# A gated recurrence and a two-layer network on one core: units 4 and 5 also run the first layer 512 columns wide, with a new order of all steps

## The chip, the cores and the metric

The kernel runs on one core of a Trainium2 chip. TensorE (PE) multiplies matrices, with its weight loads shown as an engine of their own (PEld); VectorE (DVE), ScalarE (ACT) and GpSimd (POOL) do element-wise work; SyncE (SP) issues nearly all DMAs. The metric is device time in microseconds: before the change a median of 175.93 us over 3 runs (175.39 to 175.97).

## The reference

Inputs q, k, v and f_logit have the shape (4 batches, 8 heads, 768 steps, 48). For each batch and head a 48 x 48 state is kept, and y is read from it at each step; then a two-layer network with a leaky ReLU runs over the 3072 tokens of 384 values:

```python
f = 1.0 / (1.0 + np.exp(-f_logit))
for t in range(S):
    state = f[:, :, t, :, None] * state + np.einsum('bhd,bhe->bhde', k[:, :, t], v[:, :, t])
    y[:, :, t] = np.einsum('bhd,bhde->bhe', q[:, :, t], state)
x = y.transpose(0, 2, 1, 3).reshape(B * S, H * D)
h = x @ w_in                       # 384 -> 2048
out = np.maximum(0.01 * h, h) @ w_out   # 2048 -> 384
```

## The kernel before

Time is cut into 6 chunks of 128 steps, and the work into 12 units of 256 tokens. Units 0 to 3 are one batch each with its chunks 0 and 1; units 4 to 11 are one chunk of two batches. Units 4 and 5 are chunk 2 of the four batches, 6 and 7 chunk 3, and so on.

For each unit the following is done. f, k, q and v are loaded (in the order's short names `Lf`, `Lk`, `Lq`, `Lv`, two halves each). ACT makes the log of the gate (`ge`, `gl`), PE its cumulative sum (`cs`), ACT the decay factors for k and q (`dec`, tiles em and at). k and q are scaled by them (`k`, `q`, on DVE or POOL; the last number of the word is 0 for DVE and 1 for POOL), v is cast (`v`). k and q are turned by PE with a copy behind (`tk`, `tq`, `ck`, `cq`, units 0 to 3) or by a transposing DMA on SP's queue (`xk`, `xq`, units 4 to 11). PE makes the scores (`sc`), DVE masks them (`mk`, four for a unit, tile wm), PE mixes with v and the old state (`mx`, `ms`), and two copies bring the result to the tile xT (`xt`). The new state goes through PE (`pt`), DVE (`sf`) and POOL (`sb`).

The network follows on xT. The first layer of a unit is 8 groups `up`: each does two of 16 blocks of 128 hidden values, in 2 x 3 matmuls of 256 columns (line 523), and ACT empties the bank through the leaky ReLU into the tile gT (`pr`, line 528). For two units at once it is 16 groups `uw` of 3 matmuls of 512 columns (line 534), each with one emptying of the same 128x512 size (`pv`, line 537). Which pairs do this, `WIDE` says; units 6 to 9 do so before the change. The layout of xT and gT follows it. The second layer is four quarters `dn` of 4 matmuls for each half of a unit (line 544), a copy to one of four output buffers (`ob`) and a store (`st`). Unit 11's second half ends in two half-width parts (`dc`, line 566).

Weights are loaded as f32 in eight parts each (`WI`, `WO`) into the raw buffers of units 4 and 5, and cast (`ci`, `co`). `F` words are matmuls on zeros, which fill PE's waits at the start; `Z` and `M` words clear and make constants. PSUM has eight banks; the number behind `@` is a word's bank.

Nothing is scheduled by a planner at build time. A string of words, written out in the kernel, is the order: each engine runs its instructions in the order of these words, and waits on semaphores for what they need. So an instruction that waits holds up all that stand behind it on its engine, and a DMA that waits on SP's queue holds up all later loads and stores.

Of the kernel before, what the change touches and what calls it, by code (L numbers as in the profile page):

```python
# [704 lines left out]
```

## Time and profile before

| | us |
|---|---|
| median of 3 runs | 175.93 |
| profiled execution, whole | 176.14 |
| its span | 173.9 |
| PE busy | 166.8 |
| ACT busy | 112.3 |
| DVE busy | 84.3 |
| POOL busy | 71.2 |
| PE's idle time that waits for DVE's scaling of k, in all | 1.2 |

Busy times are of the profiled execution and leave out issuing and waiting. A busy PE isn't PE at its peak: a matmul's length in the profile holds the depth of its pipeline, and what counts for the stream is the step from one start to the next.

### The profile page before, as it was taken

The numbers are of one execution on the slowest core, as the hardware profiler recorded it, in microseconds if no ns is written. First come the engines' busy times: TensorE is split into PE (matmuls) and PEld (weight loads), VectorE is DVE, ScalarE is ACT, GpSimd is POOL, SyncE is SP. The second block draws the span as 40 slices with busy tenths as digits, with TensorE's granted clock in tenths as the row PEclk, the third lists the DMA queues.
The fourth block names the chain that finished last, engine by engine and source line by source line (L and its number), as shares of the span: only waits on it lengthen the run. The fifth ranks groups of instructions, "written<-read, shape, count | busy, mean of one in ns | idle before, by whom it ended". The sixth has DMA issues, their size and how long they took to land.

```text
span 173.9 us, 5261 instructions
## 1 busy us (share of the span) xinstructions
PE 166.8 (96%) x2163; PEld 114.3 (66%) x2167; DVE 84.3 (48%) x159; ACT 112.3 (65%) x214; POOL 71.2 (41%) x127
## 2 busy tenths in 40 slices
PE   7878899999999999999999999999999999999993
...
PEclk9999999999999999999999999999999999999999
...
GB/s 138 320 312 323 329 245 374 357 156 260 293 210 180 198 153 210 179 250 217 182 138 188 243 153 216 165 172 195 216 210 140 230 185 185 73 94 45 0 94 92
DMA packets 109192, 34.45 MB, mean 198 GB/s; under 512 B 101872, under 2 KB 108144, under 8 KB 109168
## 3 DMA queue, kind: packets, MB, share of 16 engines
...
## 4 chain that ended last, share of the span: by engine, by line
PE 89%; DVE 3%; DMA 3%; ACT 1%; issue 1%; SPq 1%; DVEq 0%; ACTq 0%
PE ps L544 35%; PE ps L523 24%; PE ps L534 12%; PE ps L419 6%; DMA k_raw<-in_k_dram 3%; PE ps L388 3%; PE ps L269 2%; PE ps L566 2%; PE ps L345 1%; PE ps L495 1%; PE ps L381 1%; PE ps L101 1%; SPq L209 1%; DVE vb L328 1%; PE ps L490 1%
## 5 line engine op out<-in xcount | busy, mean ns | idle before, releaser
L544 PE MATMUL ps<-w_out,gT 128*128 128x384 bf16 x368 | 66.1, 326 | 0.0
L544 PEld LDWEIGHTS <-gT 128*128 128x128 bf16 x368 | 34.6, 98 | 22.6
L528 ACT ACTIVATE gT<-ps 128x512 bf16<-128x512 f32 x64 | 35.6, 615 | 16.3 <-PE ps L523 15.7
L523 PE MATMUL ps<-xT,w_in 128*128 128x256 bf16 x384 | 44.4, 273 | 0.2 <-DVE w_in L175 0.2
L523 PEld LDWEIGHTS <-w_in 128*128 128x128 bf16 x384 | 37.2, 98 | 5.9 <-DVE w_in L175 0.5
L402 DVE TENSOR_TENSOR wm<-ps,ut 128x512 bf16<-128x512 f32 x32 | 19.9, 684 | 17.6 <-PE ps L388 17.4
L537 ACT ACTIVATE gT<-ps 128x512 bf16<-128x512 f32 x32 | 17.6, 615 | 6.9 <-PE ps L534 6.9
L534 PE MATMUL ps<-xT,w_in 128*128 128x512 bf16 x92 | 21.8, 379 | 0.2
L324 POOL TENSOR_TENSOR kh<-k_raw,em 128x384 bf16<-128x384 f32 (+1 forms) x8 | 10.3, 1283 | 24.2 <-DMA end<-at 12.1
L324 DVE TENSOR_TENSOR kh<-k_raw,em 128x384 bf16<-128x384 f32 (+1 forms) x8 | 8.1, 1009 | 17.0 <-DMA k_raw<-in_k_dram 11.4
L534 PEld LDWEIGHTS <-w_in 128*128 128x128 bf16 x96 | 9.3, 98 | 10.2
L515 POOL CAST sb<-sf 64x192 bf16<-64x192 f32 x40 | 14.6, 364 | 3.3 <-DVE sf L505 0.9
L307 ACT ACTIVATE em<-ps 128x384 bf16<-128x384 f32 x24 | 12.2, 508 | 4.8 <-POOL sb L515 2.0
L512 POOL TENSOR_TENSOR sf<-sf,end 128x192 f32<-128x192 f32 x12 | 8.2, 680 | 16.9 <-DVE qh L324 12.5
L553 ACT COPY osb<-ps 128x384 f32<-128x384 f32 x12 | 5.9, 499 | 14.1 <-PE ps L544 11.2
L240 ACT ACTIVATE f_raw<-f_raw 128x384 f32<-128x384 f32 (+1 forms) x16 | 11.0, 692 | 4.9 <-DMA f_raw<-in_f_logit_dram 4.9
L507 DVE TENSOR_TENSOR sf<-sf,ps 64x192 f32<-64x192 f32 x32 | 11.2, 350 | 5.5 <-POOL qh L321 2.9
L328 POOL CAST vb<-v_raw 128x768 bf16<-128x768 f32 (+1 forms) x10 | 7.6, 762 | 14.2 <-PE ps L388 8.1
L321 POOL TENSOR_TENSOR qh<-q_raw,at 128x768 bf16<-128x768 f32 x4 | 8.7, 2187 | 6.8 <-ACT at L309 4.2
L555 DVE COPY osb<-ps 128x384 f32<-128x384 f32 x11 | 6.0, 555 | 11.2 <-issue 10.1
L252 ACT ACTIVATE lf<-f_raw 128x384 bf16<-128x384 f32 (+1 forms) x16 | 11.1, 691 | 0.4
L479 DVE CAST xT<-ps 128x384 bf16<-128x384 f32 x12 | 6.6, 564 | 9.0 <-PE ps L419 8.9
...
## 6 DMA issues: line engine op xcount, KB each, us to landing
k_raw<-in_k_dram SPq DMA_DIRECT2D x24, 192.0 KB, 3.8
v_raw<-in_v_dram SPq DMA_DIRECT2D x24, 192.0 KB, 3.8
f_raw<-in_f_logit_dram SPq DMA_DIRECT2D x23, 192.0 KB, 3.9
q_raw<-in_q_dram SPq DMA_DIRECT2D x23, 192.0 KB, 4.3
out_dram<-osb SPq DMA_DIRECT2D x23, 192.0 KB, 2.7
...
```

The lines of the kernel that those rows point to most:

```text
L240: nc.scalar.activation(e[:, part], e[:, part], AF.Exp, scale=-1.0)
L252: nc.scalar.activation(dst, src, AF.Ln, bias=1.0)
L307: nc.scalar.activation(ems[j % 2][:, a], t[:, 0:H * D], AF.Exp, scale=1.0)
L324: engine(e).tensor_mul(heads(j, to[j % NR], a)[:, :, :, 0:D], raw_heads(j, x, a), decays(j, by, a))
L402: nc.vector.tensor_mul(w, src.rearrange("t (p n) -> t p n", p=P2), ut[:, None, :].to_broadcast([128, P2, 128]))
L507: nc.vector.tensor_add(sf[rows], sf[rows], new)
L515: nc.gpsimd.tensor_copy(out=sb[rows, :, y * D:y * D + D], in_=sf[rows])
L523: nc.tensor.matmul(pm[:, i, :], w_in_of(ff, kk), xT_of(j)[:, kk].rearrange("t a s -> t (a s)"), start=(kk == 0), stop=(kk == NK - 1))
L528: nc.scalar.activation(gT_of(j)[:, 2 * g:2 * g + 2, :], pm, AF.Prelu, alpha=0.01)
L534: nc.tensor.matmul(banks[bank], w_in_of(ff, kk), x[:, kk], start=(kk == 0), stop=(kk == NK - 1))
L537: nc.scalar.activation(gTs[n % 2][:, 512 * ff:512 * ff + 512], banks[st[2 * n].pop(("pw", ff))], AF.Prelu, alpha=0.01)
L544: nc.tensor.matmul(po, gT_of(j)[:, ff, 128 * a:128 * a + 128], w_out_b[ff // 2][:, ff % 2, :], start=(ff == 0), stop=(ff == NF - 1))
```

## The change

The pair of units 4 and 5 joins `WIDE`: its first layer is 16 groups of 512 columns instead of 16 groups of 2 x 256 columns for the two units, with the matching layout of its xT and gT. The whole order is another one: the same steps in another sequence, on other banks, and partly on other engines. Of the steps on DVE, ACT and POOL, DVE has four more scalings of k and two more of q than before, and POOL that many fewer; ACT casts two input weight parts fewer and one output weight part more. The fill matmuls are 22 of 512 and 5 of 256 columns (20 and 3 before). The words of units 0 to 5 that the prediction speaks of stand in the order below.

```diff
-    WIDE = (3, 4)
+    WIDE = (2, 3, 4)
...
-    Zz Af_1_1 Aq_0_0 F_9_512@6 Lf_0_0 Lf_0_1 Lk_0_1 Lk_0_0 Zb_0_1_0 Zl_2_1 Mi Lv_0_0 Zq_0_0 Lv_0_1 Mu Lq_0_1
...
+    Zz Af_0_1 Ak_0_0 F_9_512@6 Lf_0_0 Lv_0_1 Lq_0_0 Lk_0_1 Lv_0_0 Lq_0_1 Lf_1_1 Lf_2_1 Lf_1_0 Lf_2_0 Lk_1_0
...
```

The loads at the start: before, ACT's queue brings the second half of unit 1's f and the first of unit 0's q, and SP's begins with f, k and v of unit 0. Now ACT's brings the second half of unit 0's f and the first of its k, and SP's begins with f, v, q, k, v, q of unit 0; then come f of units 1 and 2, and the rest of unit 1 ahead of the first weights.

DVE at the start, between the masks of unit 0 (wm0 to wm3) and those of unit 1 (wm4 to wm7). kh and qh are scaled k and q, kT and qT their turned copies, sf the state, w_in5 a part of the input weights. Before:

```order
L398 TENSOR_TENSOR wm3_114<-ps5_144,pair_mask_152 128x512
L360 COPY qT1_110<-ps0_139 128x2x256
L328 CAST vb1_105<-v_raw1_83 128x2x4x48
L324 TENSOR_TENSOR kh1_92<-k_raw1_71,em1_98 128x2x4x48
L328 CAST vb1_105<-v_raw1_83 128x2x4x48
L398 TENSOR_TENSOR wm7_118<-ps6_145,pair_mask_152 128x512
L398 TENSOR_TENSOR wm6_117<-ps5_144,pair_mask_152 128x512
L360 COPY qT1_110<-ps2_141 128x2x256
L505 TENSOR_TENSOR sf1_120<-ps1_140,at1_102 64x192 x2
L398 TENSOR_TENSOR wm4_115<-ps4_143,pair_mask_152 128x512
L175 CAST w_in5_160<-k_raw5_75 128x768
L175 CAST w_in1_156<-k_raw4_74 128x768
```

and with the change:

```order
L324 TENSOR_TENSOR kh1_92<-k_raw1_71,em1_98 128x2x4x48 x2
L507 TENSOR_TENSOR sf0_119<-sf0_119,ps7_146 64x192 x2
L328 CAST vb1_105<-v_raw1_83 128x2x4x48
L360 COPY kT1_108<-ps3_142 128x2x256
L360 COPY qT1_110<-ps5_144 128x2x256
L398 TENSOR_TENSOR wm4_115<-ps6_145,pair_mask_152 128x512
L398 TENSOR_TENSOR wm5_116<-ps7_146,pair_mask_152 128x512
L505 TENSOR_TENSOR sf1_120<-ps0_139,at1_102 64x192 x2
L398 TENSOR_TENSOR wm6_117<-ps5_144,pair_mask_152 128x512
L175 CAST w_in1_156<-k_raw4_74 128x768
L324 TENSOR_TENSOR qh2_96<-q_raw2_78,at2_103 128x2x4x48
L398 TENSOR_TENSOR wm7_118<-ps2_141,pair_mask_152 128x512
```

Both scalings of unit 1's k, the additions to unit 0's state and a scaling of unit 2's q have come into this stretch of DVE's order; one cast of v and the cast of w_in5 have gone out of it, and the first masks of unit 1 (wm4, wm5) stand right behind the copy to qT1.

PE where unit 5's half of the pair begins its first layer, a second-layer matmul ahead of it. Before:

```order
L544 MATMUL ps1_140<-w_out7_170,gT1_134 128x384
L523 LDWEIGHTS w_in1_156
L523 MATMUL ps5_144<-xT0_131,w_in1_156 128x256
L523 LDWEIGHTS w_in1_156
L523 MATMUL ps5_144<-xT0_131,w_in1_156 128x256
```

and with the change:

```order
L544 MATMUL ps1_140<-w_out7_170,gT1_134 128x384
L534 LDWEIGHTS w_in1_156
L534 MATMUL ps4_143<-xT0_131,w_in1_156 128x512
L534 LDWEIGHTS w_in1_156
L534 MATMUL ps4_143<-xT0_131,w_in1_156 128x512
```

The rows before are unit 4's, which stands alone there; unit 5's follow later behind other work. The rows with the change read both units' columns of xT0, so both units' copies into xT0 stand ahead of them.

DVE from the last mask of unit 5 on, with its last copy to xT0 and then unit 6's k, q and v. Before:

```order
L402 TENSOR_TENSOR wm5_116<-ps5_144,ut_153 128x512
L555 COPY osb0_135<-ps7_146 128x384
L479 CAST xT0_131<-ps2_141 128x3x128
L507 TENSOR_TENSOR sf2_121<-sf2_121,ps1_140 64x192 x2
L321 TENSOR_TENSOR qh1_95<-q_raw1_77,at1_102 128x16x48
L507 TENSOR_TENSOR sf3_122<-sf3_122,ps5_144 64x192 x2
```

and with the change:

```order
L402 TENSOR_TENSOR wm7_118<-ps2_141,ut_153 128x512
L555 COPY osb0_135<-ps4_143 128x384
L555 COPY osb2_137<-ps0_139 128x384
L479 CAST xT0_131<-ps5_144 128x3x128
L507 TENSOR_TENSOR sf2_121<-sf2_121,ps3_142 64x192 x2
L555 COPY osb1_136<-ps7_146 128x384
L555 COPY osb3_138<-ps1_140 128x384
L324 TENSOR_TENSOR kh0_91<-k_raw0_70,em0_97 128x16x48
L321 TENSOR_TENSOR qh0_94<-q_raw0_76,at0_101 128x16x48
L507 TENSOR_TENSOR sf3_122<-sf3_122,ps1_140 64x192 x2
L328 CAST vb0_104<-v_raw0_82 128x16x48
```

Two output copies (osb0 of unit 2, osb2 of unit 3) now stand ahead of the copy to xT0; they write the buffers that the stores of units 0 and 1 read. Unit 6's k and v, on POOL before, are on DVE behind two more output copies.

More of the change, by code (lines that the diff above doesn't have):

```diff
@@ L667 @@
[L667 to L669 removed]
+    Zz Af_0_1 Ak_0_0 F_9_512@6 Lf_0_0 Lv_0_1 Lq_0_0 Lk_0_1 Lv_0_0 Lq_0_1 Lf_1_1 Lf_2_1 Lf_1_0 Lf_2_0 Lk_1_0
+    Lq_1_0 Lk_1_1 Lv_1_1 Lv_1_0 Lq_1_1 WI_0 WI_1 Lq_2_1 Zl_0_1 Zb_1_1_0 WI_5 Zq_0_0 Lk_2_1 WI_3 Zb_2_1_1 Mi
+    Ze_1_1 Lq_2_0 WI_2 Zb_2_0_0 Lk_2_0 Lv_2_0 Lv_2_1 WI_4 WI_6 Lf_3_0 WI_7 Zl_2_0 Zl_1_0 Lv_3_1 Lk_3_1 Lf_3_1
@@ new lines @@
+    dec_1_0 k_1_0_0 cs_1_1@5 dec_1_1 k_1_1_0 cs_2_1@6 dec_2_1 Zv_0_1 mx_0_2@0.1 xt_0_0_1 ms_0 xt_0_1_1 cs_2_0@2
+    dec_2_0 sf_0_1 v_1_1_0 tk_1_0@3 ck_1_0_0 tk_1_1@4 ck_1_1_1 q_1_0_1 tq_1_0@5 F_2_512@6 F_1_256@6 cq_1_0_0
+    sc_1_0@6.7 mk_1_0_0 mk_1_0_1 Mt v_1_0_1 pt_1_2@0.3 sf_1_0 q_1_1_1 tq_1_1@1 F_3_512@5 cq_1_1_1 sc_1_1@5.2
+    F_2_512@1 F_1_256@1 ci_0_1 WO_0 up_0_0@6 pr_0_0 mk_1_1_0 ci_1_0 up_0_1@4 WO_1 pr_0_1 sb_1_0 q_2_1_0 tq_2_1@7
+    cq_2_1_1 mk_1_1_1 mx_1_2@1.0 ms_1 xt_1_1_1 ci_5_0 WO_5 up_0_5@5 pr_0_5 k_2_1_1 tk_2_1@6 sf_1_1 sb_1_1
@@ new lines @@
+    xt_1_0_0 up_1_1@2 up_1_5@4 pr_1_5 up_1_0@7 pr_1_1 pr_1_0 ci_3_1 up_1_3@3 up_0_3@1 WO_3 pr_1_3 pr_0_3 q_2_0_0
+    tq_2_0@0 k_2_0_0 tk_2_0@5 ck_2_0_0 ci_2_1 up_1_2@4 WO_2 up_0_2@2 ck_2_1_0 sc_2_1@7.3 mk_2_1_0 mk_2_1_1
+    cq_2_0_1 sc_2_0@1.5 mk_2_0_1 v_2_1_1 pr_0_2 v_2_0_1 pt_2_2@0.6 sf_2_0 ci_4_1 up_1_4@2 pr_1_4 up_0_4@7 WO_4
+    ci_6_1 up_1_6@3 WO_6 up_0_6@5 pr_0_6 mk_2_0_0 mx_2_2@2.0 sb_0_1 xt_2_0_1 pr_0_4 sb_2_0 ms_2 ci_7_0 up_0_7@1
+    pr_0_7 WO_7 up_1_7@5 pr_1_7 xt_2_1_0 up_2_4@2 up_2_1@0 up_2_6@7 up_2_5@1 up_2_3@5 ge_3_1 gl_3_1 pr_1_2
@@ new lines @@
+    dn_1_0_2 co_6_2 Lq_5_1 Lq_5_0 ge_4_2 gl_4_2 cs_4_1@1 cs_4_0@0 dec_4_1 dec_4_0 xe_4 k_4_2_1 xk_4 co_7_0
+    dn_0_0_3 dn_1_0_3 dn_0_1_3 ob_1_0_0 ob_0_0_0 ob_0_1_0 dn_1_1_3 ob_1_1_1 pt_3_2@1.3 sf_3_0 sb_3_0 sc_3_1@0.2
+    mk_3_1_0 mk_3_1_1 sc_3_0@6.5 mk_3_0_1 mk_3_0_0 dn_2_0_2 dn_2_0_3 ge_5_2 gl_5_2 cs_5_0@1 dec_5_0 cs_5_1@0
+    dec_5_1 dn_2_1_1 dn_2_1_2 mx_3_2@2.5 xt_3_0_0 ms_3 v_4_2_1 pt_4_0@6 sf_4_0 q_4_2_1 xq_4 pt_4_1@1 sf_4_1
+    dn_2_1_3 Lf_7_0 xt_3_1_1 up_3_2@0 pr_3_2 up_3_1@2 pr_3_1 up_3_7@5 pr_3_7 k_5_2_0 xk_5 q_5_2_1 xq_5 up_3_6@6
@@ new lines @@
+    pr_3_6 sf_3_1 up_3_0@1 pr_3_0 up_3_4@0 pr_3_4 sc_4_2@2.3.5.6 mk_4_1_0 mk_4_0_0 mk_4_0_1 up_3_3@1 pr_3_3
+    dn_3_0_0@0 up_3_5@5 pr_3_5 mk_4_1_1 mx_4_2@2.1 xt_4_0_0 dn_3_0_1 dn_3_0_2 sc_5_2@3.6.5.2 mk_5_0_0 mk_5_0_1
+    mk_5_1_0 xt_4_1_1 dn_3_1_0@1 dn_3_1_1 dn_3_1_2 Lf_7_1 ge_7_2 gl_7_2 cs_7_0@3 dec_7_0 cs_7_1@6 sb_3_1
+    mk_5_1_1 dn_3_0_3 sb_4_1 Lv_5_1 Lv_5_0 v_5_2_1 mx_5_2@5.2 pt_5_0@3 xt_5_1_1 st_0_0 ob_2_0_0 st_1_0 ob_3_0_0
+    dn_3_1_3 dec_7_1 Lf_6_1 Lf_6_0 ge_6_2 gl_6_2 sb_4_0 Lq_6_0 xt_5_0_0 uw_2_3@4 uw_2_2@0 uw_2_10@2 pv_2_10
@@ new lines @@
+    uw_2_13@5 pv_2_13 uw_2_1@6 pv_2_2 uw_2_14@2 pv_2_14 pv_2_1 uw_2_12@5 pv_2_12 uw_2_0@0 pv_2_0 cs_6_0@2
+    dec_6_0 Lv_6_0 Lv_6_1 st_0_1 Lk_6_0 Lk_6_1 st_1_1 xe_5 uw_2_5@6 sf_5_0 uw_2_15@3 pv_2_15 uw_2_7@5 pv_2_7
+    cs_6_1@0 dec_6_1 Lk_7_0 ob_2_1_0 uw_2_6@7 Lk_7_1 uw_2_4@2 Lq_6_1 uw_2_8@3 Lq_7_0 Lq_7_1 uw_2_9@5 ob_3_1_0
+    st_3_1 Lf_8_1 pt_5_1@1 uw_2_11@0 pv_2_3 dn_5_0_0@4 pv_2_5 dn_4_0_0@6 pv_2_4 dn_4_1_0@2 pv_2_11 dn_5_1_0@0
+    pv_2_9 k_6_2_0 xk_6 q_6_2_0 xq_6 k_7_2_1 xk_7 sf_5_1 v_6_2_0 pt_6_1@1 pt_6_0@5 sf_6_1 sf_6_0 pv_2_6 dn_4_1_1
@@ new lines @@
+    dn_5_0_1 dn_5_1_1 dn_4_0_1 q_7_2_1 xq_7 sb_5_1 Lv_7_1 pv_2_8 dn_5_0_2 sc_6_2@7.3.1.5 dn_5_0_3 dn_5_1_2
+    dn_4_0_2 dn_5_1_3 mk_6_0_1 mk_6_0_0 mk_6_1_0 mk_6_1_1 sc_7_2@3.7.1.5 mk_7_1_0 dn_4_1_2 mk_7_1_1 dn_4_1_3
+    dn_4_0_3 ob_5_1_1 mk_7_0_0 mk_7_0_1 mx_6_2@0.1 xt_6_1_0 sb_5_0 Lf_8_0 ge_8_2 gl_8_2 Lv_7_0 v_7_2_1
+    mx_7_2@5.3 xt_7_0_0 pt_7_1@7 sf_7_1 st_2_0 ob_4_0_1 pt_7_0@6 sf_7_0 st_3_0 ob_5_0_0 cs_8_0@1 xe_6 sb_6_1
+    sb_6_0 Lf_9_0 xt_6_0_1 cs_8_1@0 Lf_9_1 xt_7_1_1 uw_3_8@3 uw_3_2@5 uw_3_7@7 uw_3_6@6 uw_3_11@4 Lv_9_1 dec_8_0
@@ new lines @@
+    uw_3_1@1 Lv_9_0 Lq_8_0 dec_8_1 uw_3_9@0 pv_3_2 uw_3_0@5 Lk_8_1 Lk_8_0 k_8_2_0 Lq_8_1 Lk_9_0 pv_3_7 uw_3_3@7
+    ge_9_2 pv_3_8 uw_3_4@3 pv_3_6 uw_3_15@6 pv_3_9 uw_3_5@0 st_2_1 pv_3_11 uw_3_14@4 xe_7 sb_7_0 Lq_9_0 Lq_9_1
+    pv_3_1 uw_3_13@1 Lk_9_1 xk_8 gl_9_2 pv_3_3 cs_9_0@7 pv_3_4 cs_9_1@3 v_9_2_0 q_8_2_0 xq_8 pv_3_0 dn_7_0_0@5
+    pv_3_5 dn_7_0_1 dn_7_1_0@0 dn_7_1_1 Lv_8_0 dec_9_0 uw_3_12@7 dec_9_1 dn_6_0_0@3 dn_6_0_1 k_9_2_0 xk_9
+    q_9_2_1 xq_9 pv_3_15 pt_9_1@6 sb_7_1 Lv_8_1 v_8_2_1 pv_3_13 uw_3_10@1 pv_3_14 dn_6_1_0@4 dn_6_1_1 ob_4_1_0
@@ new lines @@
+    st_4_0 pv_3_12 Lf_10_0 sf_9_1 st_5_0 pv_3_10 sc_8_2@2.7.1.6 mk_8_0_0 mk_8_0_1 dn_7_1_2 mk_8_1_1 mk_8_1_0
+    dn_7_0_2 dn_7_0_3 dn_6_0_2 dn_6_0_3 ob_6_0_1 sc_9_2@2.7.6.1 mk_9_0_0 mk_9_1_0 mk_9_0_1 mk_9_1_1 dn_6_1_2
+    dn_6_1_3 mx_8_2@3.2 xt_8_0_1 xt_8_1_0 mx_9_2@6.7 xt_9_1_1 xt_9_0_0 dn_7_1_3 Lf_10_1 ge_10_2 gl_10_2 pt_8_1@1
+    sf_8_1 uw_4_12@3 pv_4_12 uw_4_13@2 pv_4_13 Lq_10_0 uw_4_10@7 cs_10_1@6 dec_10_1 uw_4_6@1 pv_4_6 uw_4_5@3
+    pv_4_5 st_4_1 cs_10_0@2 dec_10_0 Lq_11_0 Lq_10_1 uw_4_0@6 pv_4_0 uw_4_8@1 pv_4_8 uw_4_9@3 pv_4_9 st_6_0
@@ new lines @@
+    uw_4_2@2 pv_4_2 uw_4_3@6 pv_4_3 pt_9_0@1 sf_9_0 uw_4_14@3 pv_4_14 uw_4_11@2 pv_4_11 uw_4_1@6 pt_8_0@1 sf_8_0
+    Lv_10_1 uw_4_7@3 uw_4_4@2 Lf_11_1 Lf_11_0 ge_11_2 Lq_11_1 uw_4_15@1 Lk_10_1 Lk_11_1 Lk_10_0 Lv_10_0 st_5_1
+    xe_8 sb_8_0 Lk_11_0 ob_6_1_0 st_6_1 pv_4_1 dn_8_0_0@6 dn_8_1_0@4 pv_4_10 dn_9_1_0@7 gl_11_2 sb_8_1 pv_4_7
+    cs_11_0@3 q_10_2_0 xq_10 k_10_2_0 xk_10 pv_4_4 dn_9_1_1 cs_11_1@2 dn_8_0_1 dn_8_0_2 dn_8_1_1 dn_9_1_2
+    dn_8_1_2 dec_11_0 dn_9_0_0@3 dn_9_0_1 dn_9_0_2 ob_7_1_0 st_7_1 v_10_2_0 dec_11_1 k_11_2_0 xk_11 q_11_2_0
@@ new lines @@
+    xq_11 ob_7_0_0 st_7_0 pv_4_15 sc_10_2@0.2.1.5 mk_10_0_0 mk_10_0_1 mk_10_1_0 mk_10_1_1 dn_8_1_3 ob_8_1_1
+    st_8_1 dn_9_1_3 ob_9_1_1 st_9_1 dn_8_0_3 ob_8_0_0 mx_10_2@0.4 xt_10_1_1 sc_11_2@2.1.7.5 mk_11_0_1 mk_11_1_0
+    mk_11_1_1 mk_11_0_0 dn_9_0_3 xt_10_0_1 up_10_5@6 pr_10_5 up_10_0@4 pr_10_0 up_10_6@0 pr_10_6 up_10_7@1
+    up_10_4@7 pr_10_4 up_10_2@5 pr_10_2 up_10_1@6 pr_10_1 up_10_3@2 pr_10_3 dn_10_0_0@4 dn_10_0_1 dn_10_0_2
+    dn_10_1_0@0 dn_10_1_1 dn_10_1_2 Lv_11_1 Lv_11_0 v_11_2_1 st_8_0 xe_9 sb_9_0 sb_9_1 mx_11_2@7.5 xt_11_0_0
```

82 lines of the change are left out of this document (15 added, 67 removed).

## The prediction

> **What bounds the kernel now.** I read the page first, then TensorE's waits, then a table of stretches, and then the timelines of TensorE (PE), VectorE (DVE) and the DMA queue at the places that the change touches. From the page:
>
> ```profile
> span 173.9 us, 5261 instructions
> ...
> PE 166.8 (96%) x2163; PEld 114.3 (66%) x2167; DVE 84.3 (48%) x159; ACT 112.3 (65%) x214; POOL 71.2 (41%) x127
> ...
> PE   7878899999999999999999999999999999999993
> ...
> PEclk9999999999999999999999999999999999999999
> ...
> PE 89%; DVE 3%; DMA 3%; ACT 1%; issue 1%; SPq 1%; DVEq 0%; ACTq 0%
> ```
>
> The chain of waits lies on PE for 89% of the span, the granted clock is full, and PE's slices are below nine tenths only in the first five and in the last. A table of stretches, of which these columns are PE, weight loads, DVE, ACT, POOL, shows who is busy where PE is not:
>
> ```profile
> 10.00:15.00 5.00, 4.42 (x106) 3.14 (x108) 4.70 (x12) 3.52 (x9) 3.27 (x6) 1.00 1.09 291
> 15.00:20.00 5.00, 4.24 (x148) 3.09 (x124) 4.94 (x11) 3.58 (x8) 2.68 (x4) 1.00 1.11 359
> 20.00:25.00 5.00, 4.76 (x112) 3.82 (x111) 4.82 (x10) 3.53 (x7) 3.57 (x6) 1.00 1.00 256
> 25.00:30.00 5.00, 5.00 (x90) 4.22 (x88) 2.61 (x6) 4.60 (x10) 1.81 (x3) 1.00 1.02 353
> ```
>
> From 10 to 25 us DVE sets the pace (14.46 of 15 us); from 25 us on PE is full until the tail, as its slices on the page say. So two things can change the time: PE's total work, and how soon the start hands PE its stream. Any hole made after 25 us is pure loss, since there is no idle time of PE left to win back.
>
> **The change, term by term.**
>
> *Streaming 512 columns for units 4 and 5.* The groups, with shapes kept apart (busy us, mean ns of one | idle time before):
>
> ```profile
> L523 PE MATMUL ps<-xT,w_in 128*128 128x256 bf16 x384 | 44.4, 273 | 0.2 <-DVE w_in L175 0.2
> L523 PEld LDWEIGHTS <-w_in 128*128 128x128 bf16 x384 | 37.2, 98 | 5.9 <-DVE w_in L175 0.5
> L528 ACT ACTIVATE gT<-ps 128x512 bf16<-128x512 f32 x64 | 35.6, 615 | 16.3 <-PE ps L523 15.7
> L537 ACT ACTIVATE gT<-ps 128x512 bf16<-128x512 f32 x32 | 17.6, 615 | 6.9 <-PE ps L534 6.9
> ```
>
> and four lines of PE's timeline (start, length, instruction, count):
>
> ```profile
> 73.12 5.40 PE L523 MATMUL ps<-xT,w_in 128*128 128x256 bf16 x48
> 78.36 2.76 PE L544 MATMUL ps<-w_out,gT 128*128 128x384 bf16 x16
> ...
> 107.89 2.75 PE L534 MATMUL ps<-xT,w_in 128*128 128x512 bf16 x12
> 110.47 2.76 PE L544 MATMUL ps<-w_out,gT 128*128 128x384 bf16 x16
> ```
>
> The means (273 ns) include the pipeline's depth, so the price is the step from start to start: 48 matmuls of 256 columns in 78.36 - 73.12 = 5.24 us are 109 ns each, 12 of 512 in 110.47 - 107.89 = 2.58 us are 215 ns each. The change replaces 96 by 48: 96 x 0.109 - 48 x 0.215 = 10.46 - 10.32 = **0.1 us less**. The 48 weight loads that go (98 ns each) lie under the matmuls already: a pair of load and matmul takes 109 ns, not 98 + 109. ScalarE (ACT) empties the same 32 banks of 128x512 at the same 615 ns, so nothing is gained there.
>
> *The start.* PE's timeline up to the end of unit 1's mixing (the first and the last of three first-layer groups among them):
>
> ```profile
> 18.50 0.42 PE L381 MATMUL ps<-qT,kT 48*64 48x128 bf16 x16 [0.30 <-DVE qT L360]
> ...
> 19.30 0.82 PE L523 MATMUL ps<-xT,w_in 128*128 128x256 bf16 x6
> ...
> 21.23 0.82 PE L523 MATMUL ps<-xT,w_in 128*128 128x256 bf16 x6
> 21.98 0.81 PE L419 MATMUL ps<-wm,vb 64*32 64x128 bf16 x64
> ...
> 23.01 0.40 PE L345 MATMUL ps<-ident,kh 128*128 128x128 bf16 x4
> ```
>
> and DVE's for the same time:
>
> ```profile
> 12.12 2.49 DVE L398 TENSOR_TENSOR wm<-ps,pair_mask 128x512 bf16<-128x512 f32 x4
> 14.69 0.42 DVE L360 COPY qT<-ps 128x512 bf16<-128x512 bf16 x1
> 15.03 0.35 DVE L328 CAST vb<-v_raw 128x384 bf16<-128x384 f32 x1
> 15.29 1.36 DVE L324 TENSOR_TENSOR kh<-k_raw,em 128x384 bf16<-128x384 f32 x1
> ...
> 18.37 0.73 DVE L505 TENSOR_TENSOR sf<-ps,at 64x192 f32<-64x192 f32 x2
> ...
> 19.74 1.02 DVE L175 CAST w_in<-k_raw 128x768 bf16<-128x768 f32 x2
> 20.68 0.68 DVE L398 TENSOR_TENSOR wm<-ps,pair_mask 128x512 bf16<-128x512 f32 x1
> ```
>
> Now, from the first mask of unit 0 (12.12) to the end of the last of unit 1 (20.68 + 0.68 = 21.36), DVE works 9.24 us almost without a pause. In the changed order the same stretch holds the same eight masks, but one more scaling of k (0.996 us, the mean of its row below), one of q (0.723), one more pair of state additions (0.73), one cast of v less (0.35) and one cast of w_in less (0.51): 9.24 + 1.59 = 10.83 us. It also has one wait that was not there: the masks of unit 1's first half now stand right behind the copies that its scores need, so DVE idles for one block of 16 score matmuls, 0.42 us in its row, say 0.45. That is 11.3 us. The means, from the groups:
>
> ```profile
> L324 DVE TENSOR_TENSOR kh<-k_raw,em 128x384 bf16<-128x384 f32 x4 | 4.0, 996 | 4.9 <-DMA k_raw<-in_k_dram 4.9
> L324 DVE TENSOR_TENSOR qh<-q_raw,at 128x384 bf16<-128x384 f32 x4 | 2.9, 723 | 1.7 <-ACT at L313 1.7
> ```
>
> and for what starts the stretch, a line of the SP queue's timeline and one of the page's DMA issues (median us to landing at its end):
>
> ```profile
> 2.89 1.37 SPq L209 DMA_DIRECT2D v_raw<-in_v_dram  x2
> ```
>
> ```profile
> q_raw<-in_q_dram SPq DMA_DIRECT2D x23, 192.0 KB, 4.3
> ```
>
> The stretch begins sooner, though. Unit 0's second half of f no longer waits behind a gate of unit 1, and the whole first unit goes ahead of the others. What decides is DVE's scaling of q's second half. That load is now the sixth on the SP queue, where the second of two v loads stands today, issued at about 3.5 us; with 4.3 us to landing that is 7.8, say 8.0. Behind it on DVE come the scaling (0.72), three copies of transposes (some 0.4 each) and a pair of state multiplications (0.73): masks from 8.0 + 0.72 + 1.25 + 0.73 = 10.7, say 10.8. So the last mask of unit 1 ends at 10.8 + 11.3 = 22.1, and the mixing matmuls start there instead of at 21.98. Mixing and its state part end at about 23.2 instead of 23.01: 0.2 later. Before them PE has now done three first-layer groups (18 matmuls), in the changed order two and one set of transposes: 6 x 0.109 = 0.65 behind, 0.22 ahead. Together PE is **0.6 us behind**, and from there both orders give it an unbroken stream. Bounds: a scaling of k without POOL beside it is nearer half a microsecond than one, and masks from 10.6, give 0.5 us ahead; casts and scalings that each meet a POOL instruction (the 1.36 us row) give 1.4 us behind. I take the middle, since the row means come from the same mixture.
>
> *Units 4 and 5 together.* The pair needs both inputs before its first matmul, so unit 5 is needed where unit 4's first layer is today, at about 74 to 75 us, instead of at 85.9. Lines of PE's timeline, and of DVE's:
>
> ```profile
> 81.06 0.62 PE L388 MATMUL ps<-qT,kT 48*128 48x128 bf16 x16
> ...
> 85.89 4.09 PE L523 MATMUL ps<-xT,w_in 128*128 128x256 bf16 x36
> ```
>
> ```profile
> 73.44 1.20 DVE L328 CAST vb<-v_raw 128x768 bf16<-128x768 f32 x1
> ...
> 81.79 2.48 DVE L402 TENSOR_TENSOR wm<-ps,ut 128x512 bf16<-128x512 f32 x4 [7.15 <-PE ps L388]
> ...
> 86.92 2.30 DVE L321 TENSOR_TENSOR qh<-q_raw,at 128x768 bf16<-128x768 f32 x1 [0.76 <-issue]
> ```
>
> Counting PE's work by the steps above, its scores come at about 70 and its masks end 3.2 us later (81.06 to 84.27 today), its mixing at 73.4: there the order leaves no hole. It is tighter behind: unit 6's scalings of k and q and its cast of v now stand on DVE, one after another, ahead of its state matmuls. From the last decay factors that is 1.0 + 2.30 + 0.73 + 1.20 = 5.2 us, and those factors come 1.2 us after the cumulative sum; PE's cover from that sum to the state matmuls is four wide groups of 0.65, two short state blocks and four second-layer quarters of 0.65, about 6.0. So they come 0.4 us late. I put the later holes at **0.4 us**, bounds 0 (the casts meet no POOL work) and 1.5 (several such places).
>
> *The tail* ends as today in four quarters of a half-width output, a copy and a store: 0. Sum: -0.1 + 0.6 + 0.4 = +0.9 us. The profiled execution took 176.14 us (173.9 of it the span), so 177.0; the median of the runs is 175.93, 0.2 lower, which gives **176.8**.
>
> **Rivals.**
>
> *The start gains.* The masks begin 1.3 us sooner, and one k scaling leaves POOL for DVE. If DVE runs its added work at the lower bound and the later places are covered, the change gains 0.5 + 0.1 = 0.6, and with the wait for the scores hidden as well, 1.1: 174.8 to 175.3. For it speaks that DVE's casts and scalings are partly slowed by POOL today (1.36 against a mean of 0.996); against it, that DVE gets 1.6 us more to do exactly where it is the bound.
>
> *Unit 5 comes late (slower).* On DVE its last copy into xT now stands behind the output copies of units 2 and 3, and these wait for stores of units 0 and 1 to leave the same output buffers. Those stores are issued on SP behind unit 5's two transposes and three loads. What such issues and landings take, from SP's timeline and the page:
>
> ```profile
> 65.08 2.05 SPq L213 DMA_DIRECT2D v_raw<-in_v_dram  x2
> ```
>
> ```profile
> out_dram<-osb SPq DMA_DIRECT2D x23, 192.0 KB, 2.7
> ```
>
> By the order, DVE scales unit 5's k behind three copies and additions that follow unit 3's mixing at 60, so until about 63; its two transpositions are then issued by 65.7 (both an estimate from PE's count and DVE's means). The loads take about 1 us each to issue, the stores leave at 68.5 and 69.2 and land 2.7 later, at 71.9. DVE asks at about 73. Beyond 1.1 us of delay on the queue PE stands still one for one, with nothing behind it: at 3 us late the loss is 1.9 on top of 0.5, 178.3.
>
> *Weight loads are not as hidden as the steps say.* Halving 48 of them then saves up to 48 x 0.098 = 4.7 us: 171.2. Against it stand the 109 ns steps. The Trainium skill (TensorE: Matmul & The Clock Gate, Part 3, The mechanism) says that a weight load overlaps a running matmul only when their row groups differ, and ours all use every row; the trace disagrees. The same page (Back-to-back issue gap) gives about 131 ns a matmul as the sustained rate at 512 columns; by that figure 48 would take 6.3 us and the sum would fall by 4.2, but here the row says 215.
>
> **How the numbers follow.** About 0.5% (0.9 us) is what a measurement of this kernel can tell from no change. The start behind and PE full after it or nearly so, a loss of 0 to 1.6 us: 0.60, of which 0.30 are beyond 0.5%. Unit 5 late: 0.12, all slower. The start gains: 0.26, most of it too small to tell, 0.14 faster. Weight loads: 0.02, faster. So faster 0.16, same 0.42, slower 0.42. The likeliest case's own range is 175.9 to 177.6; with one in ten left out on each side, 175.1 to 178.5.
>
> **What would show it.** Steps right: first-layer rows of 48 wide matmuls at 215 ns; masks of unit 0 from about 10.8 and unit 1's last mask ending at about 22; PE without idle time from 25 us on, except some tenths ahead of unit 6's state matmuls. Wrong: unit 1's mixing before 21.5 (the start gains), PE idle before unit 4 and 5's first wide group and DVE there waiting for a store (unit 5 late), or wide steps well below 215 ns.

## The result, and the profile after

| | before | changed |
|---|---|---|
| median of the runs, us | 175.95 (175.39 to 175.97) | 179.95 (179.21 to 180.31) |
| profiled execution, us | 176.14 | 180.18 |
| its span, us | 173.9 | 178.4 |
| ratio to before | | 1.024 (95% interval 1.0216 to 1.0263) |

The change made the kernel 4.0 us slower, where 0.9 were forecast. From the page of the changed kernel:

```profile
span 178.4 us, 5176 instructions
...
PE 168.6 (94%) x2117; PEld 110.7 (62%) x2123; DVE 94.6 (53%) x177; ACT 111.2 (62%) x210; POOL 62.2 (35%) x113
...
PE   7599789999999999999969999999999999999993
...
PEclk9969999999999999999999999999999999999999
...
PE 78%; DVE 8%; DMA 5%; issue 3%; POOL 2%; SPq 1%; ACT 1%; DVEq 0%; POOLq 0%
```

PE has deeper dents at the start and a new one in the 21st slice, and PEclk shows something that the page of before did not: the granted clock falls to 0.6 in a slice near 10 us. DVE is busy 94.6 us instead of 84.3, POOL 62.2 instead of 71.2. The table of stretches (columns as in the prediction; the third number from the right is the granted clock, 1.00 being full) places the first dent:

```profile
5.00:10.00 5.00, 3.19 (x34) 2.36 (x33) 4.59 (x9) 3.48 (x9) 3.58 (x9) 0.83 1.17 323
10.00:15.00 5.00, 5.00 (x130) 3.86 (x128) 4.61 (x10) 4.68 (x12) 1.30 (x4) 0.83 1.12 329
15.00:20.00 5.00, 3.59 (x117) 2.67 (x94) 4.33 (x8) 3.33 (x9) 3.80 (x6) 1.00 1.05 324
```

From 10 to 15 us PE is full, but its mean clock there is only 0.83, and filling matmuls are part of what it does. Its timeline at both places (start, length, instruction, count, idle time before):

```profile
8.47 0.58 PE L345 MATMUL ps<-ident,kh 128*128 128x128 bf16 x4 [1.44 <-DVE kh L324]
...
10.55 0.82 PE L490 MATMUL ps<-vb,kh 64*128 64x96 bf16 x16
...
19.03 0.42 PE L381 MATMUL ps<-qT,kT 48*64 48x128 bf16 x16 [1.41 <-DVE qT L360]
...
23.44 0.83 PE L523 MATMUL ps<-xT,w_in 128*128 128x256 bf16 x6 [0.82 <-DVE w_in L175]
...
24.42 0.82 PE L419 MATMUL ps<-wm,vb 64*32 64x128 bf16 x64
...
85.45 2.75 PE L534 MATMUL ps<-xT,w_in 128*128 128x512 bf16 x12
88.04 0.33 PE L495 MATMUL ps<-vb,kh 128*128 128x96 bf16 x4
...
93.02 0.50 PE L495 MATMUL ps<-vb,kh 128*128 128x96 bf16 x8 [1.40 <-DVE vb L328]
```

Unit 1's mixing starts at 24.42 instead of 21.98, 2.44 later, with one first-layer group fewer done (0.65) and one set of transposes ahead (0.22): PE is 2.87 us behind. Unit 6's state matmuls wait 1.40 more, all of it for one cast of v on DVE. Together 4.3, less the 0.1 that the wide stream saves: within a few tenths the 4.0 that were measured. DVE's timeline says why, at both places:

```profile
5.53 1.24 DVE L328 CAST vb<-v_raw 128x384 bf16<-128x384 f32 x1
...
7.03 2.07 DVE L324 TENSOR_TENSOR kh<-k_raw,em 128x384 bf16<-128x384 f32 x2
9.02 0.55 DVE L324 TENSOR_TENSOR qh<-q_raw,at 128x384 bf16<-128x384 f32 x1
...
12.18 2.48 DVE L398 TENSOR_TENSOR wm<-ps,pair_mask 128x512 bf16<-128x512 f32 x4
14.58 1.82 DVE L324 TENSOR_TENSOR kh<-k_raw,em 128x384 bf16<-128x384 f32 x2
...
17.09 1.11 DVE L328 CAST vb<-v_raw 128x384 bf16<-128x384 f32 x1
...
22.13 1.25 DVE L175 CAST w_in<-k_raw 128x768 bf16<-128x768 f32 x1
...
23.77 0.68 DVE L398 TENSOR_TENSOR wm<-ps,pair_mask 128x512 bf16<-128x512 f32 x1
...
86.62 0.96 DVE L324 TENSOR_TENSOR kh<-k_raw,em 128x768 bf16<-128x768 f32 x1 [1.83 <-ACT em L307]
87.92 2.58 DVE L321 TENSOR_TENSOR qh<-q_raw,at 128x768 bf16<-128x768 f32 x1 [0.34 <-DMA q_raw<-in_q_dram]
...
91.18 1.79 DVE L328 CAST vb<-v_raw 128x768 bf16<-128x768 f32 x1
```

Beside them stands POOL's timeline:

```profile
4.78 0.78 POOL L119 MEMSET sb<- 128x384 bf16 x2
...
5.52 0.79 POOL L119 MEMSET sb<- 128x384 bf16 x2
6.23 0.33 POOL L108 MEMSET kh<- 128x256 bf16 x1
...
16.98 1.00 POOL L324 TENSOR_TENSOR qh<-q_raw,at 128x384 bf16<-128x384 f32 x1
...
89.58 2.97 POOL L321 TENSOR_TENSOR qh<-q_raw,at 128x768 bf16<-128x768 f32 x1 [0.50 <-DMA out_dram<-osb]
```

Each long cast of v ends 0.2 to 0.4 us after the POOL work beside it: the first at 6.77, POOL's clearing at 6.56; the second at 18.20, POOL's scaling at 17.98; unit 6's at 92.97, POOL's scaling at 92.55. The masks and the copies, which read PSUM (the on-chip memory that PE writes its results to), keep their 0.68 and 0.42 throughout.

### The profile page after: what moved, and what is told of

Its sections match the earlier page's. It is cut to its first block, busy times and chain, and to the rows that moved or that the text cites. A ratio compares the mean times of both kernels' runs of the same rounds, so it can differ in the third digit from the quotient of the medians.

```text
span 178.4 us, 5176 instructions
## 1 busy us (share of the span) xinstructions
PE 168.6 (94%) x2117; PEld 110.7 (62%) x2123; DVE 94.6 (53%) x177; ACT 111.2 (62%) x210; POOL 62.2 (35%) x113
## 4 chain that ended last, share of the span: by engine, by line
PE 78%; DVE 8%; DMA 5%; issue 3%; POOL 2%; SPq 1%; ACT 1%; DVEq 0%; POOLq 0%
PE ps L544 33%; PE ps L523 16%; PE ps L534 14%; PE ps L419 5%; PE ps L388 2%; DMA k_raw<-in_k_dram 2%; DVE wm L398 2%; DMA q_raw<-in_q_dram 2%; PE ps L345 2%; DVE kh L324 2%; PE ps L566 1%; PE ps L381 1%; PE ps L495 1%; PE ps L269 1%; DVE sf L507 1%
## 5 line engine op out<-in xcount | busy, mean ns | idle before, releaser
L523 PE MATMUL ps<-xT,w_in 128*128 128x256 bf16 x288 | 34.0, 273 | 0.9 <-DVE w_in L175 0.8
L534 PE MATMUL ps<-xT,w_in 128*128 128x512 bf16 x138 | 32.7, 379 | 0.3
L523 PEld LDWEIGHTS <-w_in 128*128 128x128 bf16 x288 | 27.5, 98 | 5.4 <-DVE w_in L175 1.1
L534 PEld LDWEIGHTS <-w_in 128*128 128x128 bf16 x144 | 13.8, 98 | 15.3
L515 POOL CAST sb<-sf 64x192 bf16<-64x192 f32 x40 | 15.8, 395 | 9.4 <-DVE sf L505 7.1
L324 DVE TENSOR_TENSOR kh<-k_raw,em 128x384 bf16<-128x384 f32 (+1 forms) x12 | 11.3, 952 | 14.7 <-ACT em L307 12.2
L553 ACT COPY osb<-ps 128x384 f32<-128x384 f32 x8 | 3.8, 480 | 20.8 <-PE ps L544 20.8
L555 DVE COPY osb<-ps 128x384 f32<-128x384 f32 x15 | 8.0, 552 | 13.0 <-PE ps L544 7.6
L324 POOL TENSOR_TENSOR kh<-k_raw,em 128x384 bf16<-128x384 f32 (+1 forms) x4 | 5.4, 1360 | 26.4 <-PE ps L534 10.5
L512 POOL TENSOR_TENSOR sf<-sf,end 128x192 f32<-128x192 f32 x12 | 6.4, 532 | 23.1 <-PE ps L534 14.6
L477 ACT CAST xT<-ps 128x384 bf16<-128x384 f32 x14 | 7.1, 531 | 9.2 <-PE ps L419 9.1
L479 DVE CAST xT<-ps 128x384 bf16<-128x384 f32 x10 | 5.7, 568 | 11.1 <-PE ps L419 10.8
```

The source lines that it names most:

```text
L324: engine(e).tensor_mul(heads(j, to[j % NR], a)[:, :, :, 0:D], raw_heads(j, x, a), decays(j, by, a))
L515: nc.gpsimd.tensor_copy(out=sb[rows, :, y * D:y * D + D], in_=sf[rows])
L523: nc.tensor.matmul(pm[:, i, :], w_in_of(ff, kk), xT_of(j)[:, kk].rearrange("t a s -> t (a s)"), start=(kk == 0), stop=(kk == NK - 1))
L534: nc.tensor.matmul(banks[bank], w_in_of(ff, kk), x[:, kk], start=(kk == 0), stop=(kk == NK - 1))
```

## The experiments

The theory: the order lost the time, not the wide stream; at the start through DVE instructions that stand still beside POOL and through the clock, in the middle through one cast. The rivals stand with each run. Words are those of the order string; an engine number at a word's end is 0 for DVE, 1 for POOL. All medians stand against 175.5 to 175.7 us for the kernel before in the same calls.

### Units 4 and 5 narrow again

```diff
-    WIDE = (2, 3, 4)
+    WIDE = (3, 4)
-    uw_2_3@4 uw_2_2@0 uw_2_10@2 pv_2_10 ...
+    up_5_1@4 up_4_1@0 up_4_5@2 pr_4_5 ...
```

> The changed kernel with units 4 and 5 streaming 256 columns again: every word stays where the change put it, only each wide group becomes a group of one of the two units on the same bank. Theory (the loss is in the order, not in the streaming): 180.0, within 0.3 of the changed kernel's 179.95, with the same idle times at the start and ahead of unit 6's state matmuls; the 48 matmuls of 512 columns that go are worth 0.1. Rival (the wide stream itself slows PE or what it reads): the time falls by more than 1, to below 179.

Measured: 179.56 (178.61 to 180.88), ratio to before 1.0232 (1.0180 to 1.0283). The median lies 0.1 below the range that was expected and above the rival's. The loss stays, so it is not the wide stream's. PE's two waits at the start are the same, but its wait for unit 6's v was 1.9 in the profiled execution. The four times lie far apart. The run on the clock, below, says part of why: the two with a granted clock of 0.99 took 180.88 and 179.76, the two with a full one 179.36 and 178.61.

### The old start

The first 229 words of the order before, up to the end of unit 2's mixing, then the changed order without them.

> The kernel before's order up to the state part of unit 2's mixing, then the changed order for all that is left (wide units 4 and 5 with it). Theory (some 2.9 us are lost in the first 35 us and 1.5 ahead of unit 6's state matmuls): the start's part goes and the other stays, 179.95 - 2.9 = 177.1, range 176.7 to 177.6; PE's first long stream of first-layer groups begins where it began before, and the 1.4 us of idle time ahead of unit 6's state matmuls are still there. Rival (the start's idle time is covered later, the loss lies in the middle): 179 or more.

Measured: 181.51 (179.86 to 183.64), by its number the rival's, by its reason neither's: the splice made holes of its own, of 1.16 and 2.16 us on PE. The larger, and what ACT waits for ahead of it:

```profile
43.52 0.32 PE L261 MATMUL ps<-lf,bu 128*128 128x192 bf16 x1 [2.16 <-ACT lf L252]
```

```profile
42.05 0.52 ACT L240 ACTIVATE f_raw<-f_raw 128x384 f32<-128x384 f32 x1 [3.79 <-DMA f_raw<-in_f_logit_dram]
```

The old queue of loads brings unit 3's f later than the changed order asks for it. PE's wait for unit 6's v was still there, 1.5, as expected. The run decides nothing on the start; it shows how little of such an order can be exchanged alone.

### Unit 6's v first

```diff
-    ... ob_3_1_0 ... k_6_2_0 xk_6 q_6_2_0 xq_6 ... sf_5_1 v_6_2_0
+    ... v_6_2_0 ob_3_1_0 ... k_6_2_0 xk_6 q_6_2_0 xq_6 ... sf_5_1
```

> The changed kernel with one word moved: unit 6's cast of v, on DVE, stands ahead of the last output copy of unit 3 instead of behind unit 6's scalings of k and q. Theory (PE waits 1.4 to 1.6 us for that cast alone, and has nothing else to do then): 179.95 - 1.5 = 178.4, range 178.2 to 178.8, and PE's wait for v at the state matmuls is gone. Rival (the time is given back behind it: unit 6's scores then wait for the transposed q): 179.3 or more, with a new wait of the score matmuls.

Measured: 178.18 (177.77 to 178.68), at the lower edge of what was expected, 0.02 outside it. DVE and PE there:

```profile
82.36 0.56 DVE L328 CAST vb<-v_raw 128x768 bf16<-128x768 f32 x1
```

```profile
90.65 0.50 PE L495 MATMUL ps<-vb,kh 128*128 128x96 bf16 x8
```

The wait is gone, nothing behind it takes its place, and the same cast that took 1.79 beside POOL takes 0.56 where POOL is idle. The gain is 1.8 by the medians and 1.5 between executions that kept their clock (177.8 here, in two of four; 179.3 below).

### The clock

```diff
-    F_1_512@6 F_1_256@6 dec_0_1 k_0_1_0 q_0_1_0 tk_0_0@2
+    F_1_512@6 F_1_256@6 dec_0_1 k_0_1_0 q_0_1_0 F_6_512@6 tk_0_0@2
```

> The changed kernel with six more filling matmuls of 512 columns ahead of unit 0's first transposes, where PE stands idle for 1.44 us, so that the granted clock is not lost; they end before the scaled k is there. Theory (the idle time costs the clock, and the half clock costs some tenths: four transposes in 0.58 instead of 0.40, the state part of 16 in 0.82 instead of 0.51, with DVE waiting 0.24 and 0.33 for them): masks of unit 0 at 11.6 instead of 12.18, clock 1.0 in the stretches from 5 to 15, and 179.95 - 0.5 = 179.4, range 179.1 to 179.7. Rival (DVE sets the pace there, and the clock is hidden): masks no earlier than 12.0 and 179.8 or more.

Measured: 179.30 (179.26 to 179.39), 0.65 less, and the four times now lie within 0.13. All four kept their clock; of the changed kernel's four only one had (179.21, with the others at 0.99). Between the two profiled executions the gain is 0.92. Stretches, and DVE's masks:

```profile
5.00:10.00 5.00, 4.40 (x52) 2.81 (x53) 4.80 (x10) 3.64 (x9) 3.58 (x9) 1.00 1.17 324
10.00:15.00 5.00, 4.89 (x157) 3.71 (x150) 4.73 (x10) 4.91 (x13) 1.96 (x5) 1.00 1.15 342
```

```profile
11.19 2.48 DVE L398 TENSOR_TENSOR wm<-ps,pair_mask 128x512 bf16<-128x512 f32 x4
```

The masks come 1.0 earlier, more than the 0.6 expected. So part of the loss was the clock, and filling PE's 1.44 us without work ahead of the first transposes kept it. Finer stretches of the changed kernel have its fall and its return:

```profile
8.00:8.50 0.50, 0.03 (x1) 0.06 (x2) 0.50 (x2) 0.00 (x0) 0.50 (x1) 0.80 1.17 324
8.50:9.00 0.50, 0.50 (x5) 0.39 (x5) 0.50 (x1) 0.00 (x0) 0.43 (x2) 0.50 1.17 323
...
11.50:12.00 0.50, 0.50 (x32) 0.45 (x24) 0.47 (x2) 0.50 (x2) 0.11 (x1) 0.79 1.19 317
```

Whether it is lost differs between executions of one kernel: the profiled one with unit 6's v first stood idle 1.21 there and kept it. The Trainium skill (TensorE: Matmul & The Clock Gate, Why this matters for your kernels) warns of idle gaps above some 3 us; here 1.44 was enough in the two executions that were profiled with such a gap, the changed kernel's and its narrow twin's.

### The old start up to unit 1, with unit 6's v first

The first 174 words of the order before, to just past unit 1's mixing, then the changed order's loads and all the rest.

> The kernel before's order up to the point where unit 2's second transposed k is copied (all of unit 1 is mixed by then), with the changed order's loads and everything else behind it, and unit 6's cast of v ahead of the last output copy of unit 3. The run with the old start up to the end of unit 2 had taken over the old queue of loads for unit 3, and lost 3.6 us waiting for them; here the loads behind the cut are the changed order's. Theory (start and v cast are all of the loss, and the wide stream is worth 0.1): 175.5 to 176.0, no measurable difference from the kernel before. Rival (the later order loses more, which the late start had covered): 176.8 or more.

Measured: 177.58 (177.23 to 177.70). By its number that is the rival's, by its reason neither's: unit 1's mixing starts at 21.50, there is no wait at unit 6 and none that counts after 35 us, but at the seam, where the changed kernel has no hole, PE waits for banks to be emptied:

```profile
27.59 0.38 PE L345 MATMUL ps<-ident,qh 128*128 128x128 bf16 x4 [0.95 <-ACT gT L528]
28.57 1.47 PE L523 MATMUL ps<-xT,w_in 128*128 128x256 bf16 x12 [0.60 <-ACT gT L528]
```

The two waits and one of 0.43 behind them are about the 1.9 us that this kernel lacks. The last kernel below starts unit 1's mixing at 21.09 within the changed order and has no such holes, so they come of the splice. The start had to be repaired from within the changed order.

### Two moves ahead of unit 1's mixing

On top of the six filling matmuls and unit 6's v first:

```diff
-    ci_0_1 WO_0 up_0_0@6 pr_0_0 mk_1_1_0 ci_1_0 up_0_1@4 WO_1 pr_0_1 sb_1_0 q_2_1_0 ... mk_1_1_1 mx_1_2@1.0
+    ci_0_1 ci_1_1 WO_0 up_0_0@6 pr_0_0 mk_1_1_0 mk_1_1_1 up_0_1@4 WO_1 pr_0_1 sb_1_0 q_2_1_0 ... mx_1_2@1.0
```

> The changed kernel with the six filling matmuls and the early cast of unit 6's v (177.8 together, by the two runs that kept their clock), and two moves on DVE ahead of unit 1's mixing: the cast of w_in's second piece goes to POOL, right behind the first, and the last mask of unit 1 stands right behind the third. Theory (DVE's queue, a cast of 1.25 us and a scaling of 0.55 ahead of that mask, sets unit 1's mixing): mixing 0.7 earlier, 177.1, range 176.8 to 177.4. Rival (PE's own work or the loads set it): 177.6 or more.

Measured: 176.91 (176.90 to 178.94), 0.9 less than 177.8. As the theory said, DVE's queue sets the mixing: it starts at 22.96, against 23.58 in the run with unit 6's v first. That is 0.6 of the 0.9; the rest was not followed up.

### POOL's clearing out of the way

On top of two filling matmuls and unit 6's v first:

```diff
-    Zb_3_1_1 Ze_2_0 v_0_1_0 Zb_1_0_1 Mo Zb_0_0_1 Zb_3_0_1 ... v_0_0_1
+    Ze_2_0 v_0_1_0 ... v_0_0_1 Zb_3_1_1 Zb_1_0_1 Mo Zb_0_0_1 Zb_3_0_1
```

> The changed kernel with unit 6's v early, two filling matmuls ahead of the first transposes, and four of POOL's clearing instructions (and the small one of ones) moved from beside DVE's first cast of v to behind POOL's cast of v. Theory (POOL's work beside it stretches DVE's cast from 0.35 to 1.24 us, and with it all that DVE does until the masks): the cast takes under 0.6, k is scaled from 6.5 instead of 7.03, masks of unit 0 at 10.7 instead of 11.2 to 11.3, 177.8 - 0.5 = 177.3, range 177.0 to 177.6. Rival (a DVE cast of that shape that reads a fresh load takes 1.2 us whatever POOL does, or the masks wait for q's load): masks at 11.2, 177.7 or more.

Measured: 177.20 (177.14 to 178.39), 0.6 less than 177.8, as expected. With both repairs together:

> The last two together: memsets later with two filling matmuls, and w_in's second piece cast on POOL with the last mask of unit 1 ahead. Theory (each takes DVE time off the same path): 177.8 - 0.5 - 0.7 = 176.6, range 176.2 to 177.0. Rival (the two are in each other's way, or one of them does nothing): 177.1 or more.

Measured: 176.31 (175.54 to 176.46), ratio to before 1.0028 (0.9997 to 1.0058). DVE in this last one, and POOL:

```profile
5.51 0.36 DVE L328 CAST vb<-v_raw 128x384 bf16<-128x384 f32 x1
...
6.43 0.56 DVE L324 TENSOR_TENSOR kh<-k_raw,em 128x384 bf16<-128x384 f32 x1 [0.34 <-ACT em L307]
7.20 1.08 DVE L324 TENSOR_TENSOR kh<-k_raw,em 128x384 bf16<-128x384 f32 x1 [0.21 <-ACT em L307]
...
10.76 2.49 DVE L398 TENSOR_TENSOR wm<-ps,pair_mask 128x512 bf16<-128x512 f32 x4
```

```profile
6.87 1.00 POOL L324 TENSOR_TENSOR qh<-q_raw,at 128x384 bf16<-128x384 f32 x1 [1.79 <-ACT at L313]
```

The cast takes 0.36 instead of 1.24, and the masks start at 10.76, the very time that the prediction had given them. The two gains add up.

### DVE's order and POOL's help within unit 1

Both start from the kernel with both repairs (176.31).

```diff
-    sf_0_1 v_1_1_0 tk_1_0@3 ck_1_0_0 ... cq_1_0_0 sc_1_0@6.7
+    tk_1_0@3 ck_1_0_0 ... cq_1_0_0 sf_0_1 v_1_1_0 sc_1_0@6.7
```

> The last kernel (both start repairs, unit 6's v early; 176.3), with unit 1's cast of v and unit 0's second pair of state additions moved on DVE from ahead of the copies of unit 1's first transposes to behind them. Theory (PE's 1.4 us of idle time ahead of unit 1's first scores is these two instructions, 1.10 and 0.73, and DVE's own idle 0.58 behind the copies goes when they fill it): PE's wait for the copied q under 0.3, mixing of unit 1 from 21.8 instead of 22.34, 176.3 - 0.55 = 175.75, range 175.4 to 176.1. Rival (DVE's total work sets the mixing whatever its order): 176.2 or more.

Measured: 175.84 (175.65 to 178.70), against 175.55 for the kernel before. As expected. The other way, from the same kernel:

```diff
-    k_1_1_0 ... v_1_1_0 ... q_1_0_1 ... q_1_1_1
+    k_1_1_0 q_1_0_0 ... v_1_1_0 q_1_1_0
```

> The kernel with both start repairs (176.3), and unit 1's two scalings of q taken from POOL and given to DVE, behind its scalings of k and its cast of v. Theory (DVE instructions that read two operands or f32 from the on-chip memory stand still while POOL works beside them: k twice 1.83 instead of 2 x 0.56, v 1.10 instead of 0.36): DVE takes on 2 x 0.56 = 1.12 and loses up to 1.45 of waiting, so unit 1's mixing is 0.3 earlier although DVE has more to do: 176.0, range 175.7 to 176.4, cast of v below 0.5. Rival (POOL's help is worth what it takes): 1.1 later, 177.2 or more.

Measured: 175.71 (175.56 to 176.96), 0.6 less than with POOL's help, the best that was expected. DVE, with two more scalings to do:

```profile
13.14 1.09 DVE L324 TENSOR_TENSOR kh<-k_raw,em 128x384 bf16<-128x384 f32 x2
14.15 0.55 DVE L324 TENSOR_TENSOR qh<-q_raw,at 128x384 bf16<-128x384 f32 x1
...
15.38 0.36 DVE L328 CAST vb<-v_raw 128x384 bf16<-128x384 f32 x1
15.66 0.55 DVE L324 TENSOR_TENSOR qh<-q_raw,at 128x384 bf16<-128x384 f32 x1
```

In the changed kernel two scalings and a cast took 1.82 + 1.11 = 2.93 us with POOL beside them; here four scalings and a cast take 13.14 to 14.70 and 15.38 to 16.21, 2.4 us. The two moves together, wide and narrow, where unit 2's transposes also move:

```diff
-    q_1_0_0 ... sf_0_1 v_1_1_0 q_1_1_0 tk_1_0@3 ck_1_0_0 ... cq_1_0_0 sc_1_0@6.7 ... tq_2_1@7 cq_2_1_1 mx_1_2@1.0 ms_1 xt_1_1_1
+    q_1_0_0 ... sf_0_1 tk_1_0@3 ck_1_0_0 ... cq_1_0_0 v_1_1_0 q_1_1_0 sc_1_0@6.7 ... mx_1_2@1.0 ms_1 tq_2_1@7 xt_1_1_1 cq_2_1_1
```

> The kernel with unit 1's scalings of q on DVE (175.7), and there the order within unit 1 changed once more: the copies of the first transposes ahead of the cast of v and the second scaling of q, so that these run while PE makes the scores (DVE's 0.58 of idle time and PE's 1.0 ahead of the scores go); and PE's transposes of unit 2's q behind unit 1's mixing instead of ahead of it, where they made it wait 0.17. Theory (DVE's path to unit 1's mixing still sets the time one for one): mixing from 21.1 instead of 21.79, 175.7 - 0.65 = 175.05, range 174.7 to 175.4, less than the kernel before's 175.55. Rival (the first pieces of w_in, loaded and cast by POOL only at about 18.5, or the loads set the mixing by now): 175.5 or more.

> The same kernel with units 4 and 5 streaming 256 columns again, each wide group becoming a group of one unit on the same bank. With the clock kept and the start repaired, runs should agree closely enough to see the wide stream by itself. Theory (48 matmuls at 215 ns instead of 96 at 109 ns, and nothing else): 0.1 slower than its twin, between 0.0 and 0.3. Rival (the weight loads that go are worth something): 1 to 4.7 slower.

Measured: 175.58 (175.46 to 176.76) wide, ratio to before 0.9997 (0.9981 to 1.0013), and 175.86 (175.49 to 177.06) narrow, 1.0019 (1.0000 to 1.0038). The mixing came at 21.09 as expected, but the time fell by 0.13 instead of 0.65. By its number that is the rival's. Of the 0.70 by which the mixing came earlier, one set of transposes (0.22) now only stands behind the mixing, and a first-layer group behind it waits 0.43 for a piece of w_in, a later one than the rival named; PE's weight loads:

```profile
25.50 0.55 PEld L523 LDWEIGHTS <-w_in 128*128 128x128 bf16 x6 [0.43 <-POOL w_in L175]
```

And DVE met POOL once more, 1.18 for a scaling that takes 0.55 alone; DVE, and POOL:

```profile
16.48 1.18 DVE L324 TENSOR_TENSOR qh<-q_raw,at 128x384 bf16<-128x384 f32 x1
```

```profile
16.34 0.91 POOL L175 CAST w_in<-f_raw 128x768 bf16<-128x768 f32 x1 [1.23 <-DMA f_raw<-in_moe_w_in_dram]
```

The repaired kernel is some 4.3 us faster than the changed one and cannot be told from the kernel before. Wide against narrow is 0.28 with intervals that overlap: 0.1 fits, and a gain of 1 to 4.7 from the weight loads does not (by the two intervals together the difference is at most some 0.8, an estimate). Part of the 0.28 need not be the stream's. Four of the narrow kernel's twelve times lie at 176.7 to 177.1 against one of the wide one's, and in one of these four, the profiled one, PE waits behind units 4 and 5, where the two orders are the same, for a scaling whose load of k came late:

```profile
115.37 0.34 PE L495 MATMUL ps<-vb,kh 128*128 128x96 bf16 x4 [0.90 <-DVE kh L324]
```

## Why the prediction was wrong, point by point

**The wide stream: right.** 12 matmuls of 512 columns step 88.04 - 85.45 = 2.59 us, 216 ns each, against the 215 of the working. Narrowing them again changed nothing that is clear of the noise, twice.

**No hole ahead of units 4 and 5, and none at the tail: right.** The wide stream of units 4 and 5 starts at 78.00 without a wait, so the rival in which unit 5 comes late did not happen.

**The start: wrong, and here lie 2.3 of the 3.1 us that were missing.** The step that failed reads "What decides is DVE's scaling of q's second half", timed from the landing of its load. The load landed at 7.95 (issued at 3.45, 4.5 us to landing), as counted. But DVE was not free: the scaling began at 9.02, behind a cast of v stretched from 0.36 to 1.24 by POOL's clearing and two scalings of k at 2.07. Then the half clock cost the copies and the state multiplications two waits (0.24 and 0.33) and PE its speed, and masks came at 12.18 instead of 10.8. The runs part these 1.4: with the clock kept masks came at 11.19, with the clearing moved as well at 10.76, so the clock was 1.0 and the clearing 0.4. That 10.76 meets the predicted 10.8 so closely is partly luck: the scaling of q began at 8.20 and took 0.85, both more than was counted, and the copies took less.

The other 1.0 lies in the stretch behind: 11.3 were predicted and 12.27 measured, a cast of v at 1.11 where the stretch of before had 0.35 and a cast of w_in at 1.25 where its rows gave 0.51, partly made up by scalings that were shorter than counted. The whole start came out 2.87 behind, where the bounds ended at 1.4.

The choice behind this was to take the middle of the bounds "since the row means come from the same mixture". The mixture belongs to an order, not to an instruction. In these traces a DVE instruction with both inputs, or a cast from f32, in the on-chip memory SBUF waits for the POOL instruction beside it and then takes most of its own time (casts of 0.36 and 0.56 ended 0.2 and 0.4 behind it); the means of two orders differ as their neighbours do. The same rows, from 5 to 25 us, of the changed kernel:

```profile
L328 DVE CAST vb<-v_raw 128x384 bf16<-128x384 f32 x2 | 2.3, 1173 | 0.0
```

and of the one in which POOL no longer scales unit 1's q:

```profile
L328 DVE CAST vb<-v_raw 128x384 bf16<-128x384 f32 x2 | 0.7, 360 | 0.0
```

Before, the mean of three was 704. The Trainium skill (SBUF — State Buffer, Who interferes with whom) states this as an exclusive lock, which whoever issues first has for the whole instruction while the other waits it out. The runs agree where one POOL instruction was met, and the rule would have priced each of these steps by its neighbour. The string of clearing does not fit it: the cast that began at 5.53 was held by clearing that began after it, the last at 6.23.

**Unit 6's v: right place, wrong size.** "They come 0.4 us late" was 1.4, within the bound of 1.5 that was given for several such places. The sum of 5.2 for k, q, state additions and v had 2.30 for q and 1.20 for v; they took 2.58 (with 0.34 ahead of it for the load) and 1.79, both beside POOL's scalings of unit 7. Alone, the cast takes 0.56; from 91.18 that would be 91.74, where PE stood ready at 93.02 - 1.40 = 91.62: all but covered, by this estimate.

**The clock** stood in no term. The prediction read a full clock on the page of before and carried it over, without asking how long PE would now stand idle ahead of its first transposes: 1.44 where it had been 0.33. It cost 0.65 by the medians.

**The rivals.** "The start gains" failed by the same neglect. "Weight loads" failed by the steps, and by the narrow twins. (By the 131 ns that this rival quotes, the sum would have fallen by 10.3 - 6.3 = 4.0, not 4.2.)
